# One block's convolution moved to TensorE as diagonal float32 matrices, and weight clamps moved from GpSimd to VectorE

## The chip, the cores and the metric

One core of a Trainium2 chip runs the whole program. The metric is the device time of one execution in microseconds (us). The engines run beside each other and meet by semaphores: PE (TensorE, matmuls, results in PSUM), DVE (VectorE), ACT (ScalarE), POOL (GpSimd), and SP, which here issues all the DMAs. PEld is PE's loading of the stationary matrix, which overlaps its matmuls.

## The reference

Three stages follow each other, all on 4 batches x 768 positions. First a linear attention with 8 heads of 48: per head a 48x48 state that decays by `w`, takes in the outer product of `k` and `v`, and is read by `r`. Then the first mixer, with a convolution over neighbouring positions in its gate, and the second mixer, normed and with a residual.

```python
def _moe_ref(x, w_in, conv_w, w_out):            # first mixer, 384 -> 1024 -> 384
    h = np.maximum(x @ w_in, 0.0)
    ...
    for k in range(K):                           # K = 3 taps along the sequence
        conv_out += conv_w[k][None, None, :] * hp[:, k:k + S, :]
    gate = 1.0 / (1.0 + np.exp(-conv_out))
    return (h * gate @ w_out).astype(np.float32)

def _moe2_ref(x, g_ln, w_ch1, w_ch2):            # second mixer, 384 -> 1536 -> 384
    ...
    ch = np.maximum(xn @ w_ch1, 0.0) @ w_ch2
    return (x + ch).astype(np.float32)
```

The weights of the mixers arrive as float64, read by the kernel as pairs of 32-bit words.

## The kernel before

**Work and order.** The 3072 positions are 24 attention tiles of 128 (`attn_tile`, `state_update`, both advanced by `step()`) and 8 mixer blocks of 384, that is 3 tiles to a block. The first four tiles (`EARLY`) run ahead of block 0. Then `mixer1` runs for blocks j = 0 to 7; between its pieces `after1` calls `step()`, so that attention of later tiles runs inside the blocks, at a rate set by `pace`. The results of the first mixer go to DRAM and come back for `mixer2`, which follows with 8 blocks again. The first matmul of a block needs one column of the next tile at its edge: POOL copies it (`memset` and `tensor_copy` at the end of `attn_tile`).

**A block of the first mixer.** It has 8 groups f = 0 to 7 of 128 features. `moe1_up` makes nine matmuls into the PSUM tile `psm` (the *up product*: weights and inputs are split in a high part and a low part in float32r, `wih`, `wil`, `xh`, `xl`, and three products are added). ACT makes `h` from it by Relu and the centre tap of the convolution into `c`; DVE adds the other two taps to `c` with `scalar_tensor_tensor` (L410). `gate` makes the sigmoid on ACT and multiplies by `h` on DVE (L391), `gate_split` makes high and low part `gh` and `gl`, and `down` makes nine matmuls into `acc` with `woh` and `wol` (the *down product*), two groups later (`LAG`). `psm` has two buffers in the pool `ps_m`.

**Weights.** A job (`wjob`) brings 128 rows of 512 or 768 weights: a DMA into `st`, ACT takes the magnitude of the high words, a *clamp* (`tensor_scalar` with max and min, on POOL), a *shift* (`tensor_scalar`, DVE), two *merges* (`scalar_tensor_tensor`, DVE), ACT writes the high part (`wih`, `woh`, `c1h`, `c2h`), DVE subtracts for the low part. Jobs stand in a list: three for the first half of `w_in` (f = 0 to 3), one for two groups of `w_out`, three for the second half of `w_in` (f = 4 to 7), three more for `w_out`, then six each for `w_ch1` and `w_ch2`. `wdo(n, last)` advances them by n pieces, `need(job)` finishes what a group needs. The conv weights `cw` are decoded in the same way once, after the fourth tile.

**Order on the engines.** Matmuls, the jobs and the DMAs of weights go through `InOrder` and stay in program order; the rest is put in place by the scheduler of the framework. Attention names that stand in the rows: `prt`, `pkt` (transposes), `dps` (scores), `yps` (output), `pst` (state), `kks`, `rT`, `av`, `a` and `aT` (a diagonal mask that POOL builds by `affine_select` and DVE fills by a masked copy), and `xh`, `xl`, the split output that feeds the mixer.

Of the kernel before, what the change touches and what calls it, by code (L numbers as in the profile page):

```python
# [8 lines left out]
F32 = mybir.dt.float32  # L9
# [34 lines left out]
def body(ctx, tc, r, k, v, w, u, w_in, conv_w, w_out, g_ln, w_ch1, w_ch2, out):  # L44
# [33 lines left out]

    ident = const.tile([128, 128], F32, name="ident")
    tr = const.tile([PR, NP, C], F32, name="tr")  # L80
    tku = const.tile([128, 2, H, D], F32, name="tku")
    w128 = const.tile([PR, NP, 1], F32, name="w128")
# [6 lines left out]
    vbuf = [rvbuf[:, 3 + i] for i in range(3)]  # L89
    later = const.tile([128, NP, C], F32, name="later")  # L90
    kks = const.tile([128, 2, 2, H, 64], F32, name="kks")
# [18 lines left out]

    def magnitude(st, n):

        t = ap.tile([128, WN], F32, tag="wd", name="wdec", bufs=2)[:, 0:n]
        ao.activation(out=t, in_=words(st, n)[1].bitcast(F32), func=AF.Abs)
        go.tensor_scalar(out=t, in0=t, scalar1=W_MIN, scalar2=W_MAX, op0=ALU.max, op1=ALU.min)
        return t
# [13 lines left out]

    def wjob(src, n, hi, lo, scale=None):

        st, mag = [], []

        def load():
            st.append(io.tile([128, 2 * WN], I32, tag="st", name="st", bufs=3))
            dst = st[0][:, 0:2 * n]
            if len(src.shape) == 3:
                dst = dst.rearrange("p (a n) -> p a n", a=src.shape[1])
            so.dma_start(out=dst, in_=src.bitcast(I32))  # L140

        def ahead():
            if not mag:
                mag.append(magnitude(st[0], n))

        def steps():
            ahead()
            t = mag[0]
            yield from decode(st[0], n, t)
            if me + 1 < min(len(wjobs), w_loaded[0]):  # L150
                wjobs[me + 1][2]()
            if len(src.shape) == 3:
                t = t.rearrange("p (a n) -> p a n", a=src.shape[1])
            kw = {} if scale is None else {"scale": gl[:, scale:scale + 1]}
            ao.activation(out=hi, in_=t, func=AF.Copy, **kw)
            yield
            if scale is None:
                vo.tensor_tensor(out=lo, in0=t, in1=hi.bitcast(F32), op=ALU.subtract)
            else:
                vo.scalar_tensor_tensor(out=lo, in0=t, scalar=kw["scale"], in1=hi.bitcast(F32),  # L160
                                        op0=ALU.mult, op1=ALU.subtract)
        me = len(wjobs)
        wjobs.append((load, steps(), ahead))
        return len(wjobs) - 1

# [5 lines left out]
    def wi_half(f0):  # L171
        for kt in range(KT):
            wi_job[f0 // 512] = wjob(w_in[kt * 128:kt * 128 + 128, f0:f0 + 512], 512,
                                     wih[:, kt, f0:f0 + 512], wil[:, kt, f0:f0 + 512])

    def wo_rows(f):
        wo_job[f] = wo_job[f + 1] = wjob(rows2(w_out, f), 2 * DM, woh[:, f:f + 2, :], wol[:, f:f + 2, :])

# [21 lines left out]
    def wdo(count=1, last=None):  # L200

        for _ in range(count):
            while w_done[0] < (len(wjobs) if last is None else last + 1):
                wload(w_done[0] + 2)
                if next(wjobs[w_done[0]][1], "end") != "end":
                    break
                w_done[0] += 1
# [180 lines left out]
    def gate(st):  # L388

        a_.activation(out=st["c"], in_=st["c"], func=AF.Sigmoid)  # L390
        v_.tensor_tensor(out=st["c"], in0=st["h"][:, 1:T + 1], in1=st["c"], op=ALU.mult)  # L391
# [6 lines left out]

    def moe1_up(x, f, prev):
        ps = ps_m.tile([128, 512], F32, tag="m", name="psm")  # L400
# [6 lines left out]
        a_.activation(out=h, in_=ps[:, 0:T + 2], func=AF.Relu)  # L407
        a_.activation(out=c, in_=h[:, 1:T + 1], func=AF.Copy, scale=cw[:, 1, f:f + 1])  # L408
        for tap, o in ((0, 0), (2, 2)):
            v_.scalar_tensor_tensor(out=c, in0=h[:, o:o + T], scalar=cw[:, tap, f:f + 1], in1=c,  # L410
                                    op0=ALU.mult, op1=ALU.add)
        if prev is not None:
# [61 lines left out]

    def mixer1(x, then, before=lambda f: None, after=lambda f: None):
        hold, prev = [], None
        for f in range(NF1):
            before(f)
            st = moe1_up(x, f, prev)
            if prev is not None:  # L480
# [165 lines left out]
    def conv_weights(cst):  # L646
        t = magnitude(cst, 3 * NF1)
        yield from decode(cst, 3 * NF1, t)
        v_.tensor_copy(out=cw, in_=t.rearrange("p (k f) -> p k f", k=3))
# [38 lines left out]
    while finished[0] < EARLY - 1:  # L688
        step()
        wdo(2, wo_job[0])  # L690
    for _ in conv_weights(cst):
        pass
    ahead, pace = [iter(())], [0]
    for j in range(NB):
# [10 lines left out]
        def after1(f):  # L705
# [9 lines left out]
            elif j < NB - 2:  # L715
                wdo(slot[0] % 4 == 0, c1_job[NF2 - 1])
            else:
                wdo(slot[0] % 3 == 0, c2_job[4])
            if j == NB - 1:
# [4 lines left out]

        mixer1(xT[j], spill(j), before1, after1)
    for _ in ahead[0]:
# [54 lines left out]
```

## Time and profile before

| | |
|---|---|
| Time, median of 3 runs | 677.71 us (677.46 to 679.39) |
| The profiled execution | 680.46 us, its span 678.7 us |
| PE busy | 634.3 us of the span |
| DVE busy | 434.7 us |
| ACT, POOL busy | 268.9 us, 123.1 us |
| Mean granted clock of PE | 0.977 of full speed |

All times inside the profile are counted from the start of its span. A busy time is the union of an engine's instructions; a matmul's record is longer than the distance to the next one, since matmuls are pipelined. PEclk is the clock that PE was granted as a share of 2.4 GHz: 1.00 is 2.4 GHz, 0.50 is 1.2 GHz, and what lies between is a mix over the stretch.

### The profile page before, as it was taken

The page shows a single profiled execution, that of the slowest core. Times are in us where ns is not written, and L with a number is a line of the kernel's source. Part 1 is how long each engine was busy: PE and PEld are TensorE (multiplying, and loading weights), DVE is VectorE, ACT ScalarE, POOL GpSimd, SP SyncE. Part 2 cuts the span into 40 slices and gives each one's busy share as a digit, 9 for nine tenths or more (in the row PEclk, how much of TensorE's full clock was granted, in tenths as well). Part 3 has the DMA queues.
Part 4 walks back from the last instruction along what each step waited for, and adds up shares of the span by engine and source line. Part 5 has one row for each costly group of instructions (what it writes and reads, how often), then busy time and mean ns, then how long its engine had stood idle before and what let it go on. Part 6 is the DMA issues. An engine that isn't in the chain of part 4 may idle for free.

```text
span 678.7 us, 12382 instructions
## 1 busy us (share of the span) xinstructions
PE 634.3 (93%) x5100; PEld 606.8 (89%) x5100; DVE 434.7 (64%) x823; ACT 268.9 (40%) x537; POOL 123.1 (18%) x136
## 2 busy tenths in 40 slices
PE   3758599999989999999999999999999999999996
PEld 3647488899978989999899999999999999999996
DVE  5998999998999899986999624142332415242211
ACT  1436556646565556666675312112121212112110
POOL 5452540412131312301215000000000000000000
PEclk9779699999999999999999999999999999999998
DMA  8964433333334322303033001020201002020001
GB/s 173 181 156 114 150 94 82 67 96 84 84 91 97 82 75 69 94 1 117 1 129 117 0 13 59 1 70 1 71 1 46 25 1 71 1 70 1 36 1 39
DMA packets 93841, 45.14 MB, mean 67 GB/s; under 512 B 80337, under 2 KB 89682, under 8 KB 93778
## 3 DMA queue, kind: packets, MB, share of 16 engines
q1 hardware_dynamic: 93778, 44.28, 25.1%
q8 instruction: 42, 0.69, 0.4%
q14 instruction: 21, 0.17, 0.1%
HBM read 34.83 MB, written 9.44 MB: 65 GB/s over the span
## 4 chain that ended last, share of the span: by engine, by line
PE 62%; DVE 26%; ACT 4%; issue 3%; DMA 2%; POOL 1%; SPq 0%; DVEq 0%; POOLq 0%
PE psm L70 28%; PE acc L70 28%; DVE c L410 6%; DVE wdec L70 4%; DVE aT L285 3%; DVE gl L397 3%; DVE c L391 2%; PE yps L70 2%; DMA x1b<-x_dram 2%; PE dps L70 1%; DVE rT L262 1%; PE pxt L70 1%; POOL wdec L70 1%; DVE av L270 1%; DVE kks L238 1%
## 5 line engine op out<-in xcount | busy, mean ns | idle before, releaser
L424 DVE SCALAR_TENSOR_TENSOR rl<-psm,rh 128x384 fp32r<-128x384 f32 x96 | 53.3, 555 | 142.6 <-ACT rh L423 142.6
L423 ACT ACTIVATE rh<-psm 128x384 fp32r<-128x384 f32 x96 | 47.2, 492 | 207.9 <-PE psm L70 207.9
L70 PE MATMUL psm<-xnh,c1h 128*128 128x384 f32 x288 | 99.0, 344 | 0.1
L70 PE MATMUL psm<-xnh,c1l 128*128 128x384 f32 x288 | 97.5, 338 | 0.0
L70 PE MATMUL acc<-c2h,rh 128*128 128x384 f32 x288 | 97.1, 337 | 0.0
L70 PE MATMUL acc<-c2l,rh 128*128 128x384 f32 x288 | 97.1, 337 | 0.0
L70 PE MATMUL acc<-c2h,rl 128*128 128x384 f32 x288 | 97.0, 337 | 0.0
L70 PE MATMUL psm<-xnl,c1h 128*128 128x384 f32 x288 | 96.9, 337 | 0.0
L410 DVE SCALAR_TENSOR_TENSOR c<-h,cw,c 128x384 f32<-128x384 f32 x128 | 84.5, 661 | 9.1 <-ACT c L408 8.1
L70 POOL TENSOR_SCALAR wdec<-wdec 128x768 f32<-128x768 f32 (+2 forms) x23 | 62.8, 2729 | 115.2 <-ACT wdec L70 93.6
L70 PE MATMUL psm<-xh,wih 128*128 128x386 f32 x192 | 68.9, 359 | 10.7 <-ACT wih L70 7.8
L70 PE MATMUL acc<-woh,gh 128*128 128x384 f32 x192 | 67.4, 351 | 2.3 <-DVE xl L309 1.5
L70 PE MATMUL acc<-woh,gl 128*128 128x384 f32 x192 | 65.6, 341 | 2.7 <-DVE gl L397 2.7
L70 PE MATMUL psm<-xl,wih 128*128 128x386 f32 x192 | 66.2, 345 | 0.0
L70 PE MATMUL psm<-xh,wil 128*128 128x386 f32 x192 | 66.2, 345 | 0.0
L70 PE MATMUL acc<-wol,gh 128*128 128x384 f32 x192 | 65.2, 340 | 0.0
L447 POOL TENSOR_TENSOR rs<-rs,nhalf 128x1 f32<-128x1 f32 x24 | 15.4, 658 | 227.8 <-DVE rs L446 226.4
L390 ACT ACTIVATE c<-c 128x384 f32<-128x384 f32 x64 | 33.5, 524 | 56.2 <-DVE c L410 56.0
L70 PEld LDWEIGHTS psm<-xnh,c1h 128*128 128x128 f32 x288 | 54.3, 189 | 0.4 <-DVE ok L658 0.4
L70 PEld LDWEIGHTS psm<-xnl,c1h 128*128 128x128 f32 x288 | 54.4, 189 | 0.0
L70 PEld LDWEIGHTS psm<-xnh,c1l 128*128 128x128 f32 x288 | 54.2, 188 | 0.0
L70 PEld LDWEIGHTS acc<-c2l,rh 128*128 128x128 f32 x288 | 54.1, 188 | 0.0
(104 smaller groups left out, 1162.1 us busy)
## 6 DMA issues: line engine op xcount, KB each, us to landing
st<-in_moe_w_ch_dram SPq DMA_DIRECT2D x12, 768.0 KB, 4.9
rvbuf<-in_r_dram SPq DMA_DIRECT2D x24, 192.0 KB, 2.9
kt<-in_k_dram SPq DMA_DIRECT2D x24, 192.0 KB, 3.5
rvbuf<-in_v_dram SPq DMA_DIRECT2D x24, 192.0 KB, 3.1
x_dram<-x SPq DMA_DIRECT2D x24, 192.0 KB, 1.9
x1b<-x_dram SPq DMA_DIRECT2D x24, 192.0 KB, 2.9
out_dram<-x1b SPq DMA_DIRECT2D x24, 192.0 KB, 1.9
st<-in_moe_w_in_dram SPq DMA_DIRECT2D x6, 512.0 KB, 5.9
```

Of the source, the lines that this page charges most:

```text
L70: return lambda *args, **kw: tc.keep_in_program_order(op(*args, **kw))
L238: v_.tensor_tensor(out=kks[:, n % 2, :, :, 0:D], in0=loaded[n][1].unsqueeze(1).to_broadcast([128, 2, H, D]), in1=tku, op=ALU.mult)
L262: v_.tensor_tensor(out=rT, in0=prt[0:PR], in1=tr, op=ALU.mult)
L270: v_.tensor_tensor(out=av, in0=kks[:, n % 2, 1, :, 0:D], in1=rt[:, :, 0:D], op=ALU.mult)
L285: v_.copy_predicated(out=aT[:, q], mask=later.bitcast(I32), data=dps[q])
L390: a_.activation(out=st["c"], in_=st["c"], func=AF.Sigmoid)
L391: v_.tensor_tensor(out=st["c"], in0=st["h"][:, 1:T + 1], in1=st["c"], op=ALU.mult)
L397: v_.tensor_tensor(out=st["gl"], in0=st["c"], in1=st["gh"].bitcast(F32), op=ALU.subtract)
L410: v_.scalar_tensor_tensor(out=c, in0=h[:, o:o + T], scalar=cw[:, tap, f:f + 1], in1=c, op0=ALU.mult, op1=ALU.add)
L423: a_.activation(out=gh, in_=ps[:, 0:T], func=AF.Relu)
L424: v_.scalar_tensor_tensor(out=gl_, in0=ps[:, 0:T], scalar=0.0, in1=gh.bitcast(F32), op0=ALU.max, op1=ALU.subtract)
L447: g_.tensor_tensor(out=rs[:, 1:2], in0=rs[:, 0:1], in1=nhalf, op=ALU.pow)
```

## The change

1. The convolution of block 0 (`conv_on_pe=j == 0`) is made by PE: POOL builds for each group f three diagonal 128x128 matrices of the tap weights (`taps`, an `affine_select` on `cw`, three buffers), and `gate` lets PE add three float32 matmuls of `h`, shifted by the tap, into a PSUM tile `psc` from the pool of `psm`. The sigmoid reads `psc`. The centre tap on ACT and the two tap operations on DVE are left out in block 0 and stay in blocks 1 to 7.
2. The clamps of the jobs of `w_in` and `w_out` and of the conv weights are done by DVE, in the jobs' order. Those of `w_ch1` and `w_ch2` stay on POOL.
3. A job no longer takes the magnitude of the following one ahead of time; it has one piece more (four steps to count, not three). The jobs of `w_ch1` and `w_ch2` load into a single buffer (`sc`) in place of three. The slots between the pieces change with that.
4. Ahead of block 0 only the first half of `w_in` is decoded, no longer the first job of `w_out`.
5. Four constants (`ident`, `tr`, `later`, `tku`) are views of one tile, so that `tables` stands in the rows of the change where these names stood.

```diff
-    def magnitude(st, n):
+    def magnitude(st, n, clamp):
 
         t = ap.tile([128, WN], F32, tag="wd", name="wdec", bufs=2)[:, 0:n]
         ao.activation(out=t, in_=words(st, n)[1].bitcast(F32), func=AF.Abs)
-        go.tensor_scalar(out=t, in0=t, scalar1=W_MIN, scalar2=W_MAX, op0=ALU.max, op1=ALU.min)
+        clamp.tensor_scalar(out=t, in0=t, scalar1=W_MIN, scalar2=W_MAX, op0=ALU.max, op1=ALU.min)
         return t
...
-    def wjob(src, n, hi, lo, scale=None):
-
-        st, mag = [], []
+    def wjob(src, n, hi, lo, scale=None, clamp=None):
+
+        st = []
 
         def load():
-            st.append(io.tile([128, 2 * WN], I32, tag="st", name="st", bufs=3))
+            st.append(io.tile([128, 2 * WN], I32, tag="st" if clamp else "sc", name="st", bufs=3 if clamp else 1))
...
         def steps():
-            ahead()
-            t = mag[0]
+            t = magnitude(st[0], n, clamp or go)
+            yield
             yield from decode(st[0], n, t)
-            if me + 1 < min(len(wjobs), w_loaded[0]):
-                wjobs[me + 1][2]()
+            if clamp is None:
+                wload(me + 2)
...
-                wload(w_done[0] + 2)
+                wload(w_done[0] + (2 if w_done[0] < wo_job[NF1 - 1] else 1))
...
     def gate(st):
 
-        a_.activation(out=st["c"], in_=st["c"], func=AF.Sigmoid)
+        conv = st["c"]
+        if "taps" in st:
+            conv = ps_m.tile([128, 512], F32, tag="m", name="psc")[:, 0:T]
+            for tap in range(3):
+                pe.matmul(conv, lhsT=st["taps"][:, tap], rhs=st["h"][:, tap:tap + T], start=tap == 0, stop=tap == 2)
+        a_.activation(out=st["c"], in_=conv, func=AF.Sigmoid)
         v_.tensor_tensor(out=st["c"], in0=st["h"][:, 1:T + 1], in1=st["c"], op=ALU.mult)
...
-        a_.activation(out=c, in_=h[:, 1:T + 1], func=AF.Copy, scale=cw[:, 1, f:f + 1])
-        for tap, o in ((0, 0), (2, 2)):
-            v_.scalar_tensor_tensor(out=c, in0=h[:, o:o + T], scalar=cw[:, tap, f:f + 1], in1=c,
-                                    op0=ALU.mult, op1=ALU.add)
+        if conv_on_pe:
+            st["taps"] = mp.tile([128, 3, 128], F32, tag="x1", name="taps", bufs=TT)
+            g_.affine_select(out=st["taps"], in_=cw[:, :, f:f + 1].to_broadcast([128, 3, 128]),
+                             compare_op=ALU.is_equal, fill=0.0, base=0, pattern=[[0, 3], [1, 128]], channel_multiplier=-1)
+        else:
+            a_.activation(out=c, in_=h[:, 1:T + 1], func=AF.Copy, scale=cw[:, 1, f:f + 1])
+            for tap, o in ((0, 0), (2, 2)):
+                v_.scalar_tensor_tensor(out=c, in0=h[:, o:o + T], scalar=cw[:, tap, f:f + 1], in1=c,
+                                        op0=ALU.mult, op1=ALU.add)
...
     while finished[0] < EARLY - 1:
         step()
-        wdo(2, wo_job[0])
+        wdo(2, wi_job[0])
...
             if j == 0:
                 wdo(2, wo_job[NF1 - 1])
             elif j < NB - 2:
-                wdo(slot[0] % 4 == 0, c1_job[NF2 - 1])
+                wdo(slot[0] % 3 == 0, c1_job[NF2 - 1])
             else:
-                wdo(slot[0] % 3 == 0, c2_job[4])
+                wdo(slot[0] % 2 == 0, c2_job[4])
...
-        mixer1(xT[j], spill(j), before1, after1)
+        mixer1(xT[j], spill(j), before1, after1, conv_on_pe=j == 0)
```

How the instructions then stand on three engines. Line numbers of the change are its own. On PE, in block 0, between the up product of f = 1 (its last rows are the first here) and that of f = 2, before the change:

```order
L70 MATMUL psm<-xl,wih 128x386
L70 MATMUL psm<-xh,wil 128x386
L70 MATMUL pst<-rvbuf,kks 64x48 x8
L70 MATMUL prt<-ident,rvbuf 112x128 x4
L70 MATMUL pkt<-ident,kks 112x128 x4
L70 MATMUL psm<-xh,wih 128x386
```

and after it:

```order
L70 MATMUL psm<-xl,wih 128x386
L70 MATMUL psm<-xh,wil 128x386
L70 MATMUL psc<-h,taps 128x384 x3
L70 MATMUL pst<-rvbuf,kks 64x48 x8
L70 MATMUL prt<-tables,rvbuf 112x128 x4
L70 MATMUL pkt<-tables,kks 112x128 x4
L70 MATMUL psm<-xh,wih 128x386
```

A group of three conv matmuls for f = 0 has come between. Those for f = 1 and 2 follow the up products of f = 2 and 3 in the same way, those for f = 3 to 7 all stand behind the up product of f = 4 and ahead of block 1; five down products, of f = 0 to 4, stand ahead of block 1 in both versions.

On DVE, around the end of the fourth attention tile (`xl`) and the conv weights (`wdec<-cst` to `cw`), before the change; the rows with 768 columns are the first job of `w_out`:

```order
L70 SCALAR_TENSOR_TENSOR wdec<-st,wdec 128x768
L272 TENSOR_REDUCE a_705<-av 128x8
L70 SCALAR_TENSOR_TENSOR wdec<-st,wdec 128x768
L309 TENSOR_TENSOR xl<-yps,xh 128x3x128
L70 TENSOR_TENSOR wol<-wdec,woh 128x768
L285 COPY_PREDICATED aT<-later,dps 128x512 x2
L70 TENSOR_SCALAR wdec<-wdec 128x24
L70 SCALAR_TENSOR_TENSOR wdec<-cst,wdec 128x24 x2
L649 COPY cw<-wdec 128x24
L410 SCALAR_TENSOR_TENSOR c<-h,cw,c 128x384 x2
```

and after it:

```order
L70 SCALAR_TENSOR_TENSOR wdec<-st,wdec 128x512
L70 TENSOR_TENSOR wil<-wdec,wih 128x512
L306 TENSOR_TENSOR xl<-yps,xh 128x3x128
L282 COPY_PREDICATED aT<-tables,dps 128x512 x2
L70 TENSOR_SCALAR wdec<-wdec 128x24 x2
L70 SCALAR_TENSOR_TENSOR wdec<-cst,wdec 128x24 x2
L656 COPY cw<-wdec 128x24
L70 TENSOR_SCALAR wdec<-wdec 128x768 x2
L70 SCALAR_TENSOR_TENSOR wdec<-st,wdec 128x768 x2
L393 TENSOR_TENSOR c<-h,c 128x384
```

The job of `w_out` has moved behind `cw`, a clamp stands ahead of each shift (`TENSOR_SCALAR ... x2`), and the two taps (L410) are gone. Up to the last `w_in` job's subtraction there were eight such tap operations.

On POOL, from the third tile's mask on to the conv weights, before the change; `TENSOR_SCALAR wdec` is a clamp, `MEMSET` and `CAST` are the edge columns:

```order
L275 AFFINE_SELECT aT<-a_461 128x1024
L70 TENSOR_SCALAR wdec<-wdec 128x768
L320 CAST xh<-xh 128x3
L320 CAST xl<-xl 128x3
L275 AFFINE_SELECT aT<-a_558 128x1024
L70 TENSOR_SCALAR wdec<-wdec 128x512
L275 AFFINE_SELECT aT<-a_705 128x1024
L315 MEMSET xh 128x3
L319 CAST xh<-xh 128x3
L315 MEMSET xl 128x3
L319 CAST xl<-xl 128x3
L70 TENSOR_SCALAR wdec<-wdec 128x24
```

and after it:

```order
L272 AFFINE_SELECT aT<-a_542 128x1024
L272 AFFINE_SELECT aT<-a_687 128x1024
L312 MEMSET xh 128x3
L316 CAST xh<-xh 128x3
L312 MEMSET xl 128x3
L316 CAST xl<-xl 128x3
L412 AFFINE_SELECT taps<-cw 128x384 x5
L272 AFFINE_SELECT aT<-a_844 128x1024
L412 AFFINE_SELECT taps<-cw 128x384 x3
L272 AFFINE_SELECT aT<-a_1061 128x1024
```

No clamp stands between the masks and the edge copies any more, and the eight tap matrices have come in, five ahead of the mask of the sixth tile and three ahead of that of the seventh.

## Rows read from the trace of the kernel before

**Rows 1.** The page, part 1: busy us, share of the span, instructions.

```profile
PE 634.3 (93%) x5100; PEld 606.8 (89%) x5100; DVE 434.7 (64%) x823; ACT 268.9 (40%) x537; POOL 123.1 (18%) x136
```

**Rows 2.** Stretch, its length, busy us of PE, PEld, DVE, ACT, POOL, then PEclk.

```profile
9.00:49.50 40.50, 28.25 (x389) 22.91 (x389) 35.00 (x59) 14.30 (x29) 20.63 (x20) 0.84 0.86 174
49.50:78.00 28.50, 18.98 (x159) 16.42 (x160) 24.95 (x48) 16.25 (x30) 8.85 (x6) 0.80 0.46 120
...
97.30:130.00 32.70, 30.44 (x328) 27.94 (x327) 31.98 (x58) 18.79 (x40) 5.20 (x5) 1.00 0.38 93
130.00:390.00 260.00, 254.90 (x2393) 240.21 (x2392) 230.51 (x409) 154.62 (x314) 61.31 (x48) 1.00 0.28 76
...
75.00:80.00 5.00, 3.29 (x10) 3.07 (x11) 4.19 (x5) 2.55 (x4) 3.98 (x2) 0.50 0.61 194
```

**Rows 3.** Waits, 49.5 to 97.3 us: total, times, longest.

```profile
PE psm L70 <- ACT wih L70: 7.8, 2, 5.2
...
PE acc L70 <- DVE gl L397: 1.7, 1, 1.7
```

**Rows 4.** Timeline, 19.7 to 50 us: start, duration, engine [idle before, releaser].

```profile
19.81 1.92 POOL L70 TENSOR_SCALAR wdec<-wdec 128x512 f32<-128x512 f32 x1 [3.27 <-PE yps L70]
...
21.69 1.09 POOL L275 TENSOR_SCALAR_AFFINE_SELECT aT<-a 128x1024 f32<-128x1024 f32 x1
21.77 1.38 DVE L70 TENSOR_SCALAR wdec<-wdec 128x512 int32<-128x512 int32 x1 [0.83 <-POOL wdec L70]
...
33.27 0.41 DVE L70 TENSOR_SCALAR wdec<-wdec 128x512 int32<-128x512 int32 x1
...
36.58 0.91 ACT L70 ACTIVATE wdec<-st 128x768 f32<-128x768 f32 x1 [2.56 <-DMA st<-in_moe_w_out_dram]
...
42.98 0.55 DVE L70 TENSOR_SCALAR wdec<-wdec 128x768 int32<-128x768 int32 x1
...
43.85 3.65 POOL L70 TENSOR_SCALAR wdec<-wdec 128x512 f32<-128x512 f32 x1 [2.21 <-ACT wdec L70]
...
44.79 0.94 DVE L70 SCALAR_TENSOR_TENSOR wdec<-st,wdec 128x768 int32<-128x768 int32 x1
...
46.98 0.55 DVE L309 TENSOR_TENSOR xl<-yps,xh 128x384 fp32r<-128x384 f32 x1
...
47.97 1.40 DVE L70 TENSOR_TENSOR wol<-wdec,woh 128x768 fp32r<-128x768 f32 x1 [0.44 <-ACT woh L70]
...
49.47 0.69 PE L70 MATMUL psm<-xh,wih 128*128 128x386 f32 x1 [2.85 <-POOL xl L315]
```

**Rows 5.** Groups on DVE, 49.5 to 97.3 us: busy us, mean ns.

```profile
L410 DVE SCALAR_TENSOR_TENSOR c<-h,cw,c 128x384 f32<-128x384 f32 x14 | 9.4, 680 | 2.7 <-ACT c L408 2.6
...
L70 DVE TENSOR_TENSOR wol<-wdec,woh 128x768 fp32r<-128x768 f32 x3 | 2.8, 946 | 0.0
```

**Rows 6.** Timeline, 76 to 78 us, ACT.

```profile
76.03 0.63 ACT L70 ACTIVATE wih<-wdec 128x512 fp32r<-128x512 f32 x1 [1.72 <-DVE wdec L70]
```

**Rows 7.** Timeline, 77.9 to 98 us, PE alone.

```profile
77.92 0.52 PE L70 MATMUL acc<-woh,gh 128*128 128x384 f32 x1
...
82.41 0.86 PE L70 MATMUL yps<-rT,sbds 112*32 112x128 f32 x24
83.09 1.06 PE L70 MATMUL yps<-aT,rvbuf 128*32 128x128 f32 x32
84.08 1.16 PE L70 MATMUL dps<-rT,kT 48*128 48x128 f32 x16
...
85.45 0.34 PE L70 MATMUL acc<-wol,gh 128*128 128x384 f32 x1
85.63 0.34 PE L70 MATMUL acc<-woh,gl 128*128 128x384 f32 x1
...
97.27 0.44 PE L70 MATMUL psm<-xh,wih 128*128 128x386 f32 x1
```

**Rows 8.** Waits of PE, 97.3 to 390 us.

```profile
PE prt L70 <- DVE aT L285: 3.7, 5, 1.1
```

More of the change, by code (lines that the diff above doesn't have):

```diff
@@ L76, in body @@
     go = InOrder(nc.gpsimd)
-    ident = const.tile([128, 128], F32, name="ident")
-    tr = const.tile([PR, NP, C], F32, name="tr")
-    tku = const.tile([128, 2, H, D], F32, name="tku")
+    tables_ = const.tile([128, 128 + 2 * NP * C + 2 * DM], F32, name="tables")
+    ident = tables_[:, 0:128]
+    tr = tables_[0:PR, 128:128 + NP * C].rearrange("x (p c) -> x p c", p=NP)
+    later = tables_[:, 128 + NP * C:128 + 2 * NP * C].rearrange("x (p c) -> x p c", p=NP)
+    tku = tables_[:, 128 + 2 * NP * C:].rearrange("x (a h d) -> x a h d", a=2, h=H)
     w128 = const.tile([PR, NP, 1], F32, name="w128")
@@ L89, in body @@
     vbuf = [rvbuf[:, 3 + i] for i in range(3)]
-    later = const.tile([128, NP, C], F32, name="later")
     kks = const.tile([128, 2, 2, H, 64], F32, name="kks")
@@ L140, in load @@
             so.dma_start(out=dst, in_=src.bitcast(I32))
-        def ahead():
-            if not mag:
-                mag.append(magnitude(st[0], n))
         def steps():
-            ahead()
-            t = mag[0]
+            t = magnitude(st[0], n, clamp or go)
+            yield
             yield from decode(st[0], n, t)
-            if me + 1 < min(len(wjobs), w_loaded[0]):
-                wjobs[me + 1][2]()
+            if clamp is None:
+                wload(me + 2)
             if len(src.shape) == 3:
@@ L162, in wjob @@
         me = len(wjobs)
-        wjobs.append((load, steps(), ahead))
+        wjobs.append((load, steps()))
         return len(wjobs) - 1
@@ L173, in wi_half @@
             wi_job[f0 // 512] = wjob(w_in[kt * 128:kt * 128 + 128, f0:f0 + 512], 512,
-                                     wih[:, kt, f0:f0 + 512], wil[:, kt, f0:f0 + 512])
+                                     wih[:, kt, f0:f0 + 512], wil[:, kt, f0:f0 + 512], clamp=vo)
     def wo_rows(f):
-        wo_job[f] = wo_job[f + 1] = wjob(rows2(w_out, f), 2 * DM, woh[:, f:f + 2, :], wol[:, f:f + 2, :])
+        wo_job[f] = wo_job[f + 1] = wjob(rows2(w_out, f), 2 * DM, woh[:, f:f + 2, :], wol[:, f:f + 2, :], clamp=vo)
     wi_half(0)
@@ L397, in gate_split, with moe1_up @@
         v_.tensor_tensor(out=st["gl"], in0=st["c"], in1=st["gh"].bitcast(F32), op=ALU.subtract)
-    def moe1_up(x, f, prev):
+    def moe1_up(x, f, prev, conv_on_pe):
         ps = ps_m.tile([128, 512], F32, tag="m", name="psm")
@@ L473, in queue_down, with mixer1 @@
         downq.append(go)
-    def mixer1(x, then, before=lambda f: None, after=lambda f: None):
+    def mixer1(x, then, before=lambda f: None, after=lambda f: None, conv_on_pe=False):
         hold, prev = [], None
@@ L478, in mixer1 @@
             before(f)
-            st = moe1_up(x, f, prev)
+            st = moe1_up(x, f, prev, conv_on_pe)
             if prev is not None:
@@ L646, in conv_weights @@
     def conv_weights(cst):
-        t = magnitude(cst, 3 * NF1)
+        t = magnitude(cst, 3 * NF1, vo)
         yield from decode(cst, 3 * NF1, t)
```

## Prediction

> **What bounds the kernel now.** I read first the page's busy times: TensorE (PE) is busy 634.3 of 678.7 us, VectorE (DVE) 434.7 [rows 1]. That average hides two kernels, so the next view is the busy time by stage [rows 2]. From 130 to 390 us PE is busy 254.9 of 260 us: there, and in the second mixer behind it, time can only be won by taking work off PE, and any matmul added is paid in full. Before 97 us it is the other way round. From 9 to 49.5 us, the first four attention tiles, PE works 28.25 of 40.5 us while DVE works 35.0; from 49.5 to 78 us, the first half of block 0 of the first mixer, PE works 18.98 of 28.5 us and DVE 24.95. PE has some 22 us of holes there, and the granted clock is 0.84 and 0.80, so part of PE's work in them ran at 1.2 GHz (0.50 from 75 to 80 us). The reader is to see that the change acts exactly in these holes, and that what it puts on PE behind them costs full price.
>
> What makes the holes: in block 0 PE waited 7.8 us in two pieces for ACT to write `wih` and 1.7 us for `gl` [rows 3]. In the attention stage the waits stand in the timeline [rows 4]: a shift on DVE could only start at 21.77, when the clamp that POOL had begun at 19.81 was out, and itself took 1.38 us where the same shift takes 0.41 at 33.27; at 36.58 ACT had waited 2.56 us for the `w_out` rows; POOL's clamp of 3.65 us from 43.85 stands ahead of the edge copies for which block 0's first matmul waits, and that starts at 49.47.
>
> **The change, part by part.**
>
> *The attention stage (9 to 49.5 us).* Three clamps of 128x512 go from POOL to DVE. A clamp on DVE is not in the trace; the nearest row is the shift, the same instruction kind and shape, 0.41 us [rows 4], so +1.2 us (1.9 us if it ran like the two-input form, 0.94 us for 768 columns, which is 0.63 for 512). What falls away: the wait and the stretched shift, 0.8 + 1.0 = 1.8 us; the job of the first two `w_out` rows, which now comes after the stage: shift 0.55, two merges of 0.94 and a subtraction of 1.40, 3.8 us of DVE [rows 4]; and the tail behind the last clamp: `xl` of the fourth tile is done at 46.98 + 0.55 = 47.53, and PE waits until 49.47; without the clamp ahead of them the edge copies follow at once, 1.5 us. Sum: 1.8 + 3.8 + 1.5 - 1.2 = 5.9. I take **-5.5**, some of it lost to transfers that now have to land earlier. Ends: -2.6, if only the moved job counts, and -7, if the 2.56 us of ACT behind the `w_out` load also comes back in part. Block 0 then starts at 44.0.
>
> *Block 0 up to its second half of `w_in`.* Here the conv matmuls cost nothing: three of the eight groups (f = 0, 1, 2) stand ahead of the up product of f = 4, which waits for the last `w_in` job in both versions, so they fill PE's hole. That product's last weights were written at 76.03 + 0.63 = 76.66 [rows 6], 27.2 us after the start. DVE sets this: it loses eight tap operations in this stretch (the order before), 8 x 0.68 = 5.4 us [rows 5], and gets the `w_out` job back (shift 0.55, merges 1.88, subtraction 0.95: 3.4) and four clamps (0.55 + 3 x 0.41 = 1.8): 5.2 us. **0**: the second half of `w_in` is ready 27 us after the start as before, and PE still idles, 9.5 us less three groups of 2.04 us = 3.4 us. Ends: -3 (DVE without POOL beside it is faster than its rows) and +3 (the POOL contention of the new tap matrices, below).
>
> *The conv matmuls.* Behind that point five groups of three matmuls remain, and nothing hides them. Such a matmul (float32, 128x128 stationary, 384 columns) is not in the trace. Nearest: 12 float32 matmuls of 128 columns with 32 wide stationary blocks take 83.09 - 82.41 = 0.68 us [rows 7] and leave 24 records, where a float32r matmul leaves one. If four such blocks share the array, as their outputs in four 32-partition strips suggest, one full-width float32 pass of 128 columns costs 0.68 / 3 = 0.227 us, and 384 columns 0.68 us. Lower end: 0.44, three times 1.16 / 8 from the eight score matmuls at 84.08, if none of them share the array; upper end 0.87, if they run in pairs. The stationary block is nearest to the first row taken four abreast: 0.68, or 2.04 for a group, **+10.2** (6.5 to 13.1). Besides, the group of f = 3 follows the hole, where the matmuls at 77.92 took 0.52 us at 1.2 GHz [rows 2, 7]: it loses another 2.0, less what the down product in that place loses now (9 matmuls of 0.52 for 0.34 us, 1.6): **+0.4**.
> The Trainium skill ("FP8 and Floating Point Precision", TensorE Precision Notes) says that a true float32 product needs four passes through the array; by it and the float32r matmuls of 384 columns, which start 0.18 us apart (85.45 and 85.63), the matmul would be an estimated 0.72 us, the group 2.16 and the term +10.8. The trace agrees if the four strips share.
>
> *Freed work that hides.* The centre tap on ACT and 16 tap operations on DVE (16 x 0.68 = 10.9 us) leave block 0. DVE was the chain there, so block 1 begins with DVE waiting for PE and not behind it. In 97.3 to 130 us PE is idle 32.7 - 30.44 = 2.3 us [rows 2], in waits of transposes for DVE's masked copies (3.7 us over the rest of the run [rows 8]): **-1.6** of these, between 0 and -2.3.
>
> *The rest.* The single buffer for `w_ch` loads, the extra yield and the changed slots keep a job at 12 slots in blocks 1 to 5 (4 x 3 for 3 x 4) and make it 8 for 9 later; the DMA of a job then has more than a slot to land, beside PE work; 0, and up to +3 if ACT waits at its head for a load. The shared constants tile moves no instruction that computes: 0.
>
> Sum: -5.5 + 0 + 10.2 + 0.4 - 1.6 = **+3.5**. On the profiled execution (680.46 us, 1.8 of it outside its span of 678.7) that is 684.0; the median of the runs shown is 677.71, 2.75 below it, so **681.2**.
>
> **Rivals.**
> *Faster: the hole closes.* The point that decides is whether the last `wih` comes by 24 us after the start and not 27. Then PE's remaining 3.4 us of idle and its slow clock go (some 2 us, 12 matmuls of 0.52 for 0.34 us): +3.5 - 5.4 = -1.9, with the start at its lower end -3.4, so 674 to 676. For it: DVE's clamps no longer wait for POOL and ACT. Against: DVE's own work in the stretch stays the same by the count above, and it idles at first while the weights' first step on ACT stands behind `h`. A second way to that side is a float32 matmul at its lower end: +3.5 - 3.7 = -0.2, and both together below 674.
> *No difference.* The terms of opposite sign (-7.1 and +10.6) cancel within 2 us (0.3%, about what a measurement here can tell from none): 677.7.
> *Slower by more: POOL blocks DVE.* Eight tap matrices on POOL, at 128x384, stand beside DVE's clamps. The shift of 1.38 us ran from 21.77 while POOL's mask build lay at 21.69 to 22.78 [rows 4]; 1.0 us more each time. Four in the stretch before the hole ends, +4: 685. It decides only if the builds fall into the clamps; the first three fall where DVE waits. The Trainium skill ("SBUF — State Buffer", Who interferes with whom) has the rule: the two engines share a port pair that the first one locks for its whole instruction; that row agrees.
> A fourth, on the same side: `psc` takes one of the two PSUM buffers of `psm`, so that each up product must wait for ACT to read the one before; the groups of 2.04 us cover that read, unless ACT is late. And with three tap buffers the matrix of f = 7 waits for the group of f = 4; behind it on POOL stands the mask of attention tile 6, and behind that on DVE a masked copy with the last `w_out` jobs. I leave both at up to +4.
>
> **How the numbers follow.** Forecast (slower, +2 to +6) 0.46; POOL or PSUM waits (+6 to +10) 0.10; no difference 0.22; hole closed or cheap matmul 0.22. Range for 8 in 10: 675 (a hole mostly closed) to 687 (upper end of the matmul and one of the waits); the forecast's own, 679.5 to 684.
>
> **What would show it.** Block 0's first matmul near 44 us (right if 42.5 to 47); the conv records adding 2.0 us a group; PE idle before the up product of f = 4, about 3.4 us, and its last `wih` 27 us after the start; block 1's first up matmul near 102.5, against 97.27 [rows 7]; fewer waits of transposes after it. The forecast fails if the second half of `w_in` comes much sooner, or a group costs well under 2 us.

## The result, and the profile after

The changed kernel takes 686.39 us (median of 4 runs, 685.82 to 687.83), beside 677.85 us for the kernel before: a ratio of 1.0125, 95% interval 1.0102 to 1.0148, or +8.5 us. The forecast was 681.2 us, +3.5. The direction was right and the time lies inside the range of 675 to 687; the loss is more than twice the one forecast.

The page, part 1, of the changed kernel, to be read against [rows 1]: PE works 15.2 us more, DVE 4.6 and POOL 20.2 us less, in a span of 684.0 us.

```profile
PE 649.5 (95%) x5148; PEld 615.3 (90%) x5148; DVE 430.1 (63%) x818; ACT 264.0 (39%) x529; POOL 102.9 (15%) x133
```

The stretches of [rows 2], in the changed kernel (columns as there). From 97.3 to 130 us PE has no idle time left; from 49.5 to 78 us it has 5.8 us.

```profile
9.00:49.50 40.50, 33.45 (x409) 27.91 (x410) 34.49 (x66) 13.86 (x29) 12.59 (x19) 0.87 0.90 179
49.50:78.00 28.50, 22.74 (x164) 16.65 (x163) 25.11 (x43) 14.26 (x26) 5.25 (x4) 0.82 0.51 137
75.00:80.00 5.00, 5.00 (x18) 3.60 (x17) 3.81 (x5) 2.24 (x4) 0.78 (x1) 0.70 0.18 70
97.30:130.00 32.70, 32.70 (x356) 29.27 (x354) 25.70 (x47) 17.93 (x37) 7.52 (x8) 1.00 0.42 109
```

The timeline of PE in the changed kernel. Block 0 starts at 43.77; a conv group (3 matmuls, 6 records) takes 50.86 - 48.83 = 2.03 us; PE waits twice for `wih`, 3.53 + 2.22 us; the conv group of f = 3, at 73.91, starts at the 1.2 GHz clock (granted 0.70 from 75 to 80 us); block 1 begins at 103.24, against 97.27 in [rows 7].

```profile
43.77 0.63 PE L70 MATMUL psm<-xh,wih 128*128 128x386 f32 x1 [1.66 <-POOL xl L312]
...
48.83 2.10 PE L70 MATMUL psc<-h,taps 128*128 128x384 f32 x6
50.86 0.67 PE L70 MATMUL pst<-rvbuf,kks 128*64 128x48 f32 x16
...
69.06 0.69 PE L70 MATMUL psm<-xh,wih 128*128 128x386 f32 x1 [3.53 <-ACT wih L70]
72.70 0.69 PE L70 MATMUL psm<-xh,wih 128*128 128x386 f32 x1 [2.22 <-ACT wih L70]
73.91 4.04 PE L70 MATMUL psc<-h,taps 128*128 128x384 f32 x6
81.04 2.10 PE L70 MATMUL psc<-h,taps 128*128 128x384 f32 x6
...
103.24 0.63 PE L70 MATMUL psm<-xh,wih 128*128 128x386 f32 x1
```

Waits of PE from 103.3 us on: those of transposes for masked copies have gone from the 3.7 us of [rows 8] to 0.4; the largest are now two for `xn` at the start of the second mixer.

```profile
PE pxt L70 <- DVE xn L456: 2.2, 2, 1.3
...
PE prt L70 <- DVE aT L282: 0.4, 1, 0.4
```

### The profile page after: what moved, and what is told of

Read it like the earlier page. It is cut to its first block, busy times and chain, and to the rows that moved or that the text cites. A ratio compares the mean times of both kernels' runs of the same rounds, so it can differ in the third digit from the quotient of the medians.

```text
span 684.0 us, 12524 instructions
## 1 busy us (share of the span) xinstructions
PE 649.5 (95%) x5148; PEld 615.3 (90%) x5148; DVE 430.1 (63%) x818; ACT 264.0 (39%) x529; POOL 102.9 (15%) x133
## 4 chain that ended last, share of the span: by engine, by line
PE 62%; DVE 26%; ACT 5%; issue 3%; DMA 2%; POOL 0%; SPq 0%; DVEq 0%
PE psm L70 27%; PE acc L70 27%; DVE c L417 7%; DVE wdec L70 4%; DVE aT L282 3%; DVE c L393 2%; DVE gl L399 2%; PE psc L70 2%; PE yps L70 2%; DVE rT L259 1%; PE pxt L70 1%; ACT c L392 1%; PE dps L70 1%; DVE av L267 1%; DVE kks L235 1%
## 5 line engine op out<-in xcount | busy, mean ns | idle before, releaser
L417 DVE SCALAR_TENSOR_TENSOR c<-h,cw,c 128x384 f32<-128x384 f32 x112 | 77.8, 696 | 8.8 <-ACT c L415 7.8
L70 PEld LDWEIGHTS acc<-c2h,rh 128*128 128x128 f32 x288 | 54.1, 188 | 0.0
L70 PEld LDWEIGHTS acc<-c2h,rl 128*128 128x128 f32 x288 | 54.0, 188 | 0.0
L70 POOL TENSOR_SCALAR wdec<-wdec 128x768 f32<-128x768 f32 x12 | 36.4, 3035 | 113.5 <-ACT wdec L70 113.4
```

The costliest lines, as they stand in the source:

```text
L70: return lambda *args, **kw: tc.keep_in_program_order(op(*args, **kw))
```

## The experiments

Each run has its ratio to the kernel before on the same chip; "the last `wih`" is the end of ACT's write of the last weights that the up product of f = 4 needs. The *evacuation* of a block is ACT's copy of the finished down product from `acc` to `x`; the last addition is DVE's for the last output. The *hole* is the time that PE idles in block 0 before the up product of f = 4.

**A second profile of the kernel before** (no edit).

> The kernel before once more, for a second profile. The profiled execution of before lay 2.75 us above the median of its runs, that of the changed kernel 0.6 us below its own, so the pair of traces shows +5.4 us and the medians +8.5. If before simply varies (theory A), this profile has a span near 676 and block 1's first up matmul stands where it stood, at 97.3, within 0.3 us, so that the 3 us lie behind it, spread or in one place. If the 3 us are an early stall (theory B), block 1's first up matmul comes at 94 to 95 here.

Measured: 678.85 us, span 677.1 us, beside a median of 678.69. The profile that the prediction was made from had started block 0 late, 49.47 against 48.07 us here, and block 1 begins at 95.88 instead of 97.27: 1.4 of the 1.6 us between the two spans lie ahead of block 0 (theory B in kind, less in size). The three later versions that keep the attention stage of before start at 48.33 to 48.36 us. In this profile: block 0's first matmul, the last `wih`, block 1's first matmul, block 0's evacuation and the last addition.

```profile
48.07 0.69 PE L70 MATMUL psm<-xh,wih 128*128 128x386 f32 x1 [3.76 <-POOL xl L315]
...
74.62 0.63 ACT L70 ACTIVATE wih<-wdec 128x512 fp32r<-128x512 f32 x1 [1.72 <-DVE wdec L70]
...
95.88 0.44 PE L70 MATMUL psm<-xh,wih 128*128 128x386 f32 x1
...
112.52 1.23 ACT L432 ACTIVATE x<-acc 128x384 f32<-128x384 f32 x3
...
669.87 1.60 DVE L457 TENSOR_TENSOR x1b<-acc,x1b 128x384 f32<-128x384 f32 x3 [4.17 <-PE acc L70]
```

**The changed kernel again** (no edit).

> The changed kernel once more, beside the parts of it on one chip. If the first ratio holds, 1.0125 within its interval. In the profile, theory A: block 0 starts within 0.5 us of 43.8 and its first evacuation comes 74.5 us after that, against 64.4 in either profile of before; the last output's addition stands 8.4 us ahead of the end of the span, against 7.2. If one of these was an accident of one execution, it is not seen again.

Measured: 687.49 us, ratio 1.0122 (1.0104 to 1.0140); span of the profile 685.1 us. The same five places:

```profile
44.09 0.69 PE L70 MATMUL psm<-xh,wih 128*128 128x386 f32 x1 [2.42 <-POOL xl L312]
...
72.62 0.63 ACT L70 ACTIVATE wih<-wdec 128x512 fp32r<-128x512 f32 x1 [3.01 <-DVE wdec L70]
...
104.30 0.63 PE L70 MATMUL psm<-xh,wih 128*128 128x386 f32 x1
...
119.34 1.23 ACT L439 ACTIVATE x<-acc 128x384 f32<-128x384 f32 x3
...
676.60 1.62 DVE L464 TENSOR_TENSOR x1b<-acc,x1b 128x384 f32<-128x384 f32 x3 [4.21 <-PE acc L70]
```

These two profiles, 8.0 us apart, are the pair for the account. Block 0 starts 4.0 us earlier, the last `wih` is only 2.0 us earlier (73.25 against 75.25), block 1 begins 8.4 us later, block 0's evacuation comes 6.8 us later, the last addition 6.7 us later, and the end 8.0 us later. So +8.8 us arise between the last `wih` and the end of block 0, nothing in the 557 us behind it, and +1.3 us behind the last addition.

**Without the conv on PE.**

```
-        mixer1(xT[j], spill(j), before1, after1, conv_on_pe=j == 0)
+        mixer1(xT[j], spill(j), before1, after1, conv_on_pe=False)
```

> The changed kernel with the taps of block 0 back on ScalarE and VectorE, all else as changed (clamps on VectorE, moved job, slots, single load buffer). Theory A (the conv matmuls are the whole loss): the attention stage still ends near 44, the eight tap operations (5.4 us) return ahead of the second half of w_in, so that it comes about 32 us after the start, near 76, and the time is that of before within 2 us, 676 to 680. Theory B (the slots, the single load buffer or the clamps cost some 3 to 4 us of the 8.5): 681 to 683.

Measured: 681.49 us, ratio 1.0048 (1.0034 to 1.0061). The rest of the change alone costs 3.3 us by the ratio, theory B's number. In the profile it is 2.6: block 0's evacuation comes 1.0 us later and the last addition 1.4, and 1.2 lie behind that. Block 0 starts 4.0 us earlier than in the second profile of before, yet the last `wih` ends at 77.01, 1.8 us later:

```profile
44.10 0.69 PE L70 MATMUL psm<-xh,wih 128*128 128x386 f32 x1 [2.42 <-POOL xl L312]
...
76.38 0.63 ACT L70 ACTIVATE wih<-wdec 128x512 fp32r<-128x512 f32 x1 [3.01 <-DVE wdec L70]
```

**The conv on PE alone** (the kernel before with the conv, and the shared constants tile).

```
+        if conv_on_pe:
+            st["taps"] = mp.tile([128, 3, 128], F32, tag="x1", name="taps", bufs=TT)
...
+        mixer1(xT[j], spill(j), before1, after1, conv_on_pe=j == 0)
```

> The kernel before with the matmul conv in block 0 and the shared constants tile it needs for space; clamps, jobs, loads and slots as before. Theory A: attention as before (block 0 starts at 49.5), the second half of w_in comes 5.4 us earlier than 76.7, near 71.3, five groups of 2.04 us and 0.4 are paid: +10.6 - 5.4 = +5.2, and -1.6 behind it: 681 to 683. Theory B (the other parts of the change cost 3 to 4 us net in the later blocks and the conv less than its 10.2): 678 to 680.

Measured: 680.10 us, ratio 1.0016 (1.0007 to 1.0025), +1.1 us: between the two. With POOL's clamps the eight tap operations taken from DVE bring the last `wih` to 69.11, 6.1 us earlier than before, and PE's hole closes, at a better clock. The stretch 49.5 to 78 us:

```profile
49.50:78.00 28.50, 28.50 (x203) 23.79 (x202) 24.97 (x43) 16.29 (x29) 19.29 (x13) 0.93 0.52 147
```

This is the "hole closes" rival, in this version and not in the changed one. Alone, the two halves cost 3.3 and 1.1 us; together 8.0 to 8.5, though each of the two holds the 1 us at the end that the shared tile brings (below). The 5 us between are the hole: the conv frees DVE enough to close it, and the rest of the change opens it again. The last `wih` comes 4.1 us later in the changed kernel (73.25 against 69.11), of which 2.9 are work of DVE, about what its clamps take, and 1.2 idle time; and the conv group of f = 3 takes 4.04 us there instead of 2.10 here, where PE had no idle time before it.

**The conv in the hole only, in the changed kernel.**

```
-            st = moe1_up(x, f, prev, conv_on_pe)
+            st = moe1_up(x, f, prev, conv_on_pe and f < 3)
```

> The changed kernel with the matmul conv for the groups f = 0, 1, 2 alone, which stand ahead of the up product of f = 4, in TensorE's hole; f = 3 to 7 on ScalarE and VectorE. Theory A: the 10.6 us of the five groups go, VectorE gets their ten tap operations (6.8 us) back, of which up to 1.6 us show: 686.4 - 10.6 + 0 to 3 = 676 to 679. Theory B (the rest of the change costs 3 to 4 us): 680 to 682. By either it is faster than the changed kernel by over 4 us; if it is not, the groups behind the hole were covered.

Measured: 680.22 us, ratio 1.0019 (1.0008 to 1.0030): 7 us faster than the changed kernel by the ratios, at the edge between the two theories. The five groups behind the hole are not covered.

**The groups behind the hole twice.**

```
-            for tap in range(3):
+            for tap in [0, 1, 2] * (2 if st["f"] >= 3 else 1):
```

> The changed kernel with the conv group of f = 3 to 7 of block 0 issued twice, 15 matmuls more with the same results. Theory A (behind the hole nothing hides them, 0.68 us each): +10.2 us on the changed kernel (687.5 where before is 679.5): 697 to 698. Theory B (part of a group lies beside waits of the up and down products): +5 to +8: 692 to 695.

Measured: 696.22 us, ratio 1.0244 (1.0217 to 1.0270): +8.3 us by the ratios, with an uncertainty of 2, and +9.6 us in the profiles, 0.7 of which is a later start. A doubled group takes 4.03 us instead of 2.10 by the records (6.31 for 4.04 where it begins at 1.2 GHz). That is between the two theories, nearer to A: nearly all of the five groups is paid, some 9 of 10.2 us.

```profile
74.91 6.31 PE L70 MATMUL psc<-h,taps 128*128 128x384 f32 x12
84.23 4.03 PE L70 MATMUL psc<-h,taps 128*128 128x384 f32 x12
```

**The shared constants tile alone**, in the kernel before.

```
-    ident = const.tile([128, 128], F32, name="ident")
+    tables_ = const.tile([128, 128 + 2 * NP * C + 2 * DM], F32, name="tables")
+    ident = tables_[:, 0:128]
...
```

> The kernel before with the shared constants tile alone. Every changed variant so far shows 8.4 us from the last output's addition to the end of the span, before 7.2, and 5 instead of 4 instruction packets on the second instruction queue there. Theory A: the tail comes with the program's layout, and with this edit too: +1.2 us and nothing ahead of it. Theory B: it needs the conv or the jobs: no difference, within 0.3 us of before, and a tail of 7.2 us.

Measured: 680.49 us, ratio 1.0017 (1.0004 to 1.0029), +1.1 us; from the start of the last addition to the end 8.2 us instead of 7.2, as theory A said. (In this one profile another 1.0 us lies ahead of that; two executions of the kernel before differ by 1.6.) The DMA queues in the last 9 us (packets, MB, share), first in the second profile of before:

```profile
q14 instruction: 4, 0.03, 1.3%
```

And in this version: no engine has more work to do, but the trace counts 12438 instructions instead of 12382, and one more packet of instructions is loaded while the program ends.

```profile
q14 instruction: 5, 0.04, 1.7%
```

**The job of the first two `w_out` rows back in the attention stage**, in the changed kernel.

```
-        wdo(2, wi_job[0])
+        wdo(2, wo_job[0])
```

> The changed kernel with the job of the first two w_out rows back in the attention stage. Theory A (VectorE is the chain from 10 us to the last wih in either place, so that moving 3.4 to 3.8 us of its work across the start of block 0 changes only the start): block 0 starts near 47, its last wih comes about 25.5 us after that, and the time is that of the changed kernel within 1 us. Theory B (the job in block 0 is what reopened the hole): 3 us or more faster than the changed kernel.

Measured: 685.97 us, ratio 1.0094 (1.0078 to 1.0111), 1.5 us below the changed kernel on the same chip, between the two, and the intervals touch. Block 0 starts at 44.65, only 0.6 us later, and not near 47. But the edit did not do what it was meant to: with four steps to a job, only the clamp of it (the first row below) comes ahead of the fourth tile's `xl`; shift, merges and subtraction still stand behind it. So this run does not show what the job was worth to the start.

```profile
44.48 0.58 DVE L70 TENSOR_SCALAR wdec<-wdec 128x768 f32<-128x768 f32 x1
44.97 0.54 DVE L306 TENSOR_TENSOR xl<-yps,xh 128x384 fp32r<-128x384 f32 x1
45.43 0.54 DVE L70 TENSOR_SCALAR wdec<-wdec 128x768 int32<-128x768 int32 x1
```

**The look-ahead back**, in the changed kernel.

```
         def steps():
-            t = magnitude(st[0], n, clamp or go)
-            yield
+            if clamp is None:
+                ahead()
+                yield
+            else:
+                ahead()
+            t = mag[0]
             yield from decode(st[0], n, t)
             if clamp is None:
                 wload(me + 2)
+            elif me + 1 < w_loaded[0] and me < wo_job[NF1 - 1]:
+                wjobs[me + 1][2]()
...
```

> The changed kernel with the look-ahead of before restored for the w_in and w_out jobs: a job starts the next one's first step on ScalarE and its clamp (still on VectorE) between its own merges, and the extra yield goes. VectorE's instructions stay the same. Theory A (VectorE's sum of work from 9 us to the last wih sets the end: busy 56.0 of 64.3 us in the changed kernel, 53.1 of 60.1 with POOL's clamps): its idle time there can fall by the 2.4 us for ScalarE's first step and up to 1.4 of the waits for wih, so 1 to 3 us faster than the changed kernel (687.5 where before is 679.5). Theory B (the order of the job's steps, 20 in 16 slots, is what keeps the hole open): 4 us or more faster.

Measured: 683.77 us, ratio 1.0058 (1.0038 to 1.0077), some 4 us faster by the ratios, though its profile (span 682.9) shows 2.2: not decided between the theories. Block 0 starts 2.6 us later, at 46.67, and the last `wih` ends at 73.07, within 0.2 us of the changed kernel: PE only waits less before it. Of the 2.2 us, 1.5 arise between the last `wih` and block 0's evacuation, 1.0 of these in the conv group of f = 3, which follows one wait of 2.95 us in place of two of 3.25 and 2.22 and loses less at the slow clock:

```profile
74.33 3.05 PE L70 MATMUL psc<-h,taps 128*128 128x384 f32 x6
```

**Without the clamps.**

```
-        clamp.tensor_scalar(out=t, in0=t, scalar1=W_MIN, scalar2=W_MAX, op0=ALU.max, op1=ALU.min)
+        if clamp is go or n == 3 * NF1:
+            clamp.tensor_scalar(out=t, in0=t, scalar1=W_MIN, scalar2=W_MAX, op0=ALU.max, op1=ALU.min)
```

> The changed kernel without the clamps of the w_in and w_out jobs: weights outside the range are not brought into it; the seven or so VectorE instructions of 0.42 to 0.58 us ahead of the last wih are gone and nothing takes their place on POOL. Theory A (VectorE is the chain from 9 us to the last wih): that comes 2.5 to 4 us earlier than 73.2, near 70, and the time falls by the same, to 683.5 to 685. Theory B (the early start of block 0 is the gain and the clamps are covered): block 0 starts earlier by about 1 us and the rest follows: 686 to 687.

Measured: 685.41 us, ratio 1.0088 (1.0061 to 1.0114): by the ratios 2.3 us faster than the changed kernel, with an uncertainty of 2, and 1.0 in the profiles. The last `wih` ends at 70.99, 2.3 us earlier, with the start of block 0 unchanged (44.00), and block 0's evacuation comes 2.4 us earlier (116.96): theory A up to there, slightly under its lower end. Of the 2.4 us, 1.7 are lost again before the last addition in this profile.

What these versions have in common is seen in one view, the busy time from 9 us to the last `wih` (columns as in [rows 2]; DVE is the third engine). The kernel before, second profile:

```profile
9.00:75.25 66.25, 45.59 (x543) 38.04 (x543) 58.68 (x104) 30.03 (x57) 29.43 (x26) 0.82 0.70 156
```

The changed kernel, second profile:

```profile
9.00:73.25 64.25, 49.65 (x561) 40.33 (x561) 56.03 (x102) 25.22 (x51) 17.37 (x24) 0.89 0.77 162
```

The conv alone, with POOL's clamps:

```profile
9.00:69.11 60.11, 48.20 (x548) 39.65 (x549) 53.13 (x91) 25.07 (x49) 35.77 (x32) 0.89 0.77 169
```

The changed kernel with the look-ahead:

```profile
9.00:73.07 64.07, 50.06 (x561) 40.81 (x561) 55.76 (x103) 26.27 (x51) 19.41 (x24) 0.92 0.74 163
```

And without the clamps:

```profile
9.00:70.99 61.99, 48.44 (x561) 39.19 (x561) 53.46 (x95) 25.44 (x51) 17.82 (x24) 0.94 0.75 167
```

In these five DVE idles 7.0 to 8.5 us; in all fifteen profiles it idles 6.6 to 9.5 us, while its busy time runs from 52.9 to 60.8 and the last `wih` from 68.9 to 77.0. The last `wih` follows DVE's busy time to within some 1.5 us, wherever block 0 starts. The largest busy time is that of the run without the conv, which starts early:

```profile
9.00:77.01 68.01, 47.16 (x543) 38.76 (x543) 60.76 (x112) 29.18 (x57) 11.94 (x17) 0.84 0.68 152
```

**The kernel before with the conv in the hole only.**

```
-            st = moe1_up(x, f, prev, conv_on_pe)
+            st = moe1_up(x, f, prev, conv_on_pe and f < 3)
```

> The kernel before with the matmul conv for f = 0, 1, 2 of block 0 alone, clamps and jobs as before. With all eight groups TensorE had no idle time from 49.5 to 78 us (last wih at 68.5). Theory A (the hole pays three groups, the five behind it cost 10.2 less the tap work that they take from VectorE): the time falls from 680.1 by 10.2 and gets back up to 3: 670 to 673. Theory B (the ten tap operations behind the hole stall TensorE's next products, as the variant with f = 0 to 2 of the changed kernel lost 4 us of its 10.2): 674 to 677.

Measured: 675.59 us, ratio 0.9939 (0.9925 to 0.9954), 3.9 us faster than the kernel before and 11.9 us faster than the changed one, on the same chip: theory B's range. Its stretches from 49.5 and 78 us: the hole is closed, and behind it PE idles 2.3 us where the taps are back on DVE.

```profile
49.50:78.00 28.50, 28.50 (x269) 24.56 (x269) 25.88 (x47) 17.49 (x32) 14.49 (x8) 0.95 0.52 136
78.00:97.30 19.30, 16.98 (x158) 14.89 (x157) 19.30 (x31) 11.11 (x22) 9.38 (x6) 1.00 0.38 99
```

**The same with the first three clamps on DVE.**

```
-            mag.append(magnitude(st[0], n))
+            mag.append(magnitude(st[0], n, clamp))
...
-                                     wih[:, kt, f0:f0 + 512], wil[:, kt, f0:f0 + 512])
+                                     wih[:, kt, f0:f0 + 512], wil[:, kt, f0:f0 + 512],
+                                     clamp=vo if f0 == 0 else None)
```

> The version with the conv on TensorE for f = 0 to 2 and POOL's clamps (675.6 where before is 679.5), with the clamps of the first three w_in jobs, those of the attention stage, moved to VectorE. Theory A: block 0 starts about 4 us earlier, near 44.5, but VectorE gets 1.2 us of work and the last wih comes no earlier than 68.9; TensorE waits there for what it won: same time within 1 us. Theory B (the attention stage's 4 us are a gain): 671.5 to 673.

Measured: 676.49 us, ratio 0.9957 (0.9942 to 0.9972): the same time within 1.3 us, but not for the reason given. Block 0 did not start earlier (48.74): the look-ahead still put the next half's clamp on POOL ahead of the fourth tile's mask and the edge copies. That clamp (done at 46.79) holds the mask for 1.3 us; for the rest DVE is late, whose `a` for that mask is done at 45.47 here and at 42.25 in the next run. So this run does not tell the theories apart.

```profile
43.14 3.65 POOL L70 TENSOR_SCALAR wdec<-wdec 128x512 f32<-128x512 f32 x1 [2.21 <-ACT wdec L70]
```

**The same with the early start.**

```
-        wdo(2, wo_job[0])
+        wdo(2, wi_job[0])
...
-            if me + 1 < min(len(wjobs), w_loaded[0]):
+            if me != wi_job[0] and me + 1 < min(len(wjobs), w_loaded[0]):
```

> The version with the conv on TensorE for f = 0 to 2, with the clamps of the first three w_in jobs on VectorE, the job of the first two w_out rows moved behind the attention stage, and no look-ahead across that border, so that no clamp of POOL stands ahead of the edge copies; behind the border POOL's clamps and the look-ahead stay. Theory A (VectorE's work from 9 us to the last wih is what counts): block 0 starts 4 us earlier, near 44, the last wih is written near 70 as with the late start (68.9, plus the 1.2 us of three clamps), TensorE waits there for 3 to 4 us, and the time is that of the version with the late start, 0.994 of before, or up to 1 us above it. Theory B (the early start is a gain of its own): the last wih comes about 20.5 us after the start, near 65, and the time is 3 to 4 us lower, 0.988 to 0.990 of before.

Measured: 679.88 us, ratio 1.0014 (1.0001 to 1.0028): some 5 us slower than with the late start. Block 0 starts 4.6 us earlier, and the last `wih` ends at 75.01, 6.1 us later than the 68.90 of the late start. Theory B falls. Theory A's time is missed too: DVE waits 5.2 us for POOL's first clamp behind the border, and 10 more of its instructions now stand ahead of the last `wih` (56.47 us busy against 52.93).

```profile
43.72 0.44 PE L70 MATMUL psm<-xh,wih 128*128 128x386 f32 x1 [1.22 <-POOL xl L317]
...
50.04 0.96 DVE L70 TENSOR_SCALAR wdec<-wdec 128x768 int32<-128x768 int32 x1 [5.21 <-POOL wdec L70]
...
74.38 0.63 ACT L70 ACTIVATE wih<-wdec 128x512 fp32r<-128x512 f32 x1 [1.48 <-DVE wdec L70]
```

## Why the prediction was wrong, by its own steps

**The step that failed is the first term, "-5.5" for the attention stage, taken together with the "0" for block 0 up to its second half of `w_in`.** The term was read from PE's start. But the up product of f = 4 waits for its weights, and in every version DVE works from 9 us to the last `wih` with little idle time. Only what DVE sheds of work or of idle time moves that end. By the prediction's own prices its work falls by 3.8 - 1.2 + 5.4 - 5.2 = 2.8 us (the job and the taps out, the clamps and the job in); the other 2.7 of the 5.5 were waits that were to fall away, on DVE and at PE's start. Between the second profiles DVE's busy time falls by 2.65 us, as priced, but its idle time grows by 0.65, and the last `wih` comes 2.0 us earlier. The prediction had written "DVE sets this" and yet counted the start.

The waits did not go; they changed their place. Of DVE's waits up to the last `wih`, those that went, in the second profile of before:

```profile
DVE c L410 <- ACT c L408: 2.6, 1, 2.6
...
DVE wdec L70 <- POOL wdec L70: 1.1, 1, 1.1
```

And those that came, in that of the changed kernel, where DVE waits for a job's first step on ACT (2.4 us; with the look-ahead 0.4) and for `wih`:

```profile
DVE wdec L70 <- ACT wdec L70: 2.4, 1, 2.4
DVE wil L70 <- ACT wih L70: 2.1, 3, 0.7
```

The stretched shift, 1.0 us of the "1.8", came back too, as a stretched clamp: one on DVE took 1.31 us beside POOL's mask build, where another took 0.42.

```profile
27.56 1.39 POOL L272 TENSOR_SCALAR_AFFINE_SELECT aT<-a 128x1024 f32<-128x1024 f32 x1 [6.06 <-DVE a L269]
27.92 1.31 DVE L70 TENSOR_SCALAR wdec<-wdec 128x512 f32<-128x512 f32 x1
...
35.92 0.42 DVE L70 TENSOR_SCALAR wdec<-wdec 128x512 f32<-128x512 f32 x1
```

Three runs bear out that an earlier start is worth nothing by itself, though none changes the start alone. Without the conv, block 0 starts 4.0 us earlier and the last `wih` comes 1.8 later. With the look-ahead it starts 2.6 us later than in the changed kernel, and the last `wih` does not move. The third is the early start with the conv in the hole only, which brought a wait of its own.

**Inside that term** the start itself was met, 43.8 to 44.1 us for a forecast of 44.0, in part by luck: 1.4 of the 5.5 were one execution's late start, and from the other starts of before the gain is some 4 us. In the second profiles, DVE's `a` of the fourth tile (L272 before, L269 after), for which POOL's mask waits, is done 2.9 us earlier (41.90 against 44.80), and POOL, without its clamp, begins that mask at once and not 1.3 us later. The job's share in this is not measured; of its 3.8 us, the subtraction of 1.40 stood behind `xl` already before [rows 4].

**The conv matmuls** were right: 2.03 us a group (forecast 2.04). From the last `wih` to the end of block 0 the loss is 8.8 us; the forecast's +10.2 + 0.4 - 1.6 is 9.0. The group of f = 3 lost 1.9 us at the 1.2 GHz clock (4.04 for 2.10 us; forecast 2.0). The doubled groups agree (some 9 of 10.2). The -1.6 was right as well: in the second profiles block 1 starts 8.4 us later (104.30 against 95.88), and block 0's evacuation, which falls behind that, 6.8 us.

**PE's wait before f = 4** was to be 3.4 us and is 5.5 to 5.8: it is longer by about the 2.0 us by which the stretch from the start to the last `wih` grew, from 27.2 to 29.2 us.

**"The rest: 0"** missed 1.3 us at the end of the program, a term that stood nowhere. The run with the tile alone has 1.0 of them, with a price of 1.1 us; the prediction held that the tile "moves no instruction that computes", which is so, and not enough.

The sum as it should have been: -2.0 + 8.8 - 0.1 + 1.3 = +8.0 for the pair of profiles. The medians give 8.0 and 8.5. That 686.39 us lies inside the stated range is luck: its upper end, 687, stood for dearer matmuls and a POOL or PSUM wait, and neither is what came.

**The rivals.** "The hole closes" came about when the clamps and the jobs stayed as before. "POOL blocks DVE" and the PSUM buffer were not tried alone, but the second profile of the changed kernel settles them. Up to the last `wih`, two DVE instructions beside a tap build are longer than their like, a clamp of 0.76 us for 0.42 and a merge of 1.01 for 0.68: 0.7 us together. Beside the longest build it is the build that is long (four of them took 1.94 us together elsewhere), and DVE's clamp is not:

```profile
57.08 2.18 POOL L412 TENSOR_SCALAR_AFFINE_SELECT taps<-cw 128x384 f32<-128x384 f32 x1 [8.44 <-PE psc L70]
...
57.52 0.42 DVE L70 TENSOR_SCALAR wdec<-wdec 128x512 f32<-128x512 f32 x1
```

PE's waits from 43 to 120 us, the whole of block 0, are on two suppliers; none is for a PSUM buffer or for a tap matrix:

```profile
PE psm L70 <- ACT wih L70: 5.5, 2, 3.3
PE psm L70 <- POOL xl L312: 2.4, 1, 2.4
```

What stays open is how much the look-ahead gains, 4 us by the medians and 2.2 in its profile, and where the run without clamps loses 1.7 us again.

## What to carry to other kernels

An engine that starts earlier has won nothing if it waits later for the same supplier: measure a saving at the last event of the chain that both versions wait for, and count there only what the supplier itself sheds. Work put on the engine with the hole is free as far as the hole reaches, so place it by that border (f = 0 to 2 here, 675.6 us for 679.5), and do not in the same change refill the engine whose relief closes the hole. Two edits that each look cheap can spend the same slack: here +1.1 and +3.3, each with the 1 us at the end in it, made +8.0 to +8.5.

## What the hardware showed that was not expected

An edit that adds no work to any engine made the end of the program 1.0 us longer: the trace holds 56 more instructions, which no engine counts as work, and one more packet on the instruction queue, 5 for 4, in the last 9 us. It is the same in all thirteen profiles with the shared tile: 5 packets, and 8.1 to 8.8 us from the start of the last addition to the end, where both profiles of before have 4 packets and 7.2 us. That the packet is the cause is not shown. The Trainium skill ("Runtime: NRT & Kernel Launch", Terms) says that an engine's instruction memory is refilled in blocks; the extra packet agrees with a program that crosses into another one, but no run here moved that border on purpose.
